# First up weights in two halves, weight blocks 4 to 7 one column at a time, and the deviation of two columns by a square root and a reciprocal

## The chip, the cores and the metric

The kernel runs on one core of a Trainium2 chip. The metric is the time on the device in microseconds (us), as the median of several runs. A profiled execution gives the trace of every instruction and DMA. The engines are TensorE (PE, matmuls; its weight loads are listed as PEld), VectorE (DVE), ScalarE (ACT), GpSimd (POOL) and SyncE (SP, which here only issues DMAs). Each engine works through its own instructions in the order of the program and waits at semaphores for the others.

## What is computed

A row of 512 numbers is normalised, and three things are added: the input, a spectral filter (a two-dimensional real FFT over 2048 rows and 512 columns, a product with a complex weight, and the inverse), and a gated feed-forward layer with 1792 hidden units. Cut to what matters:

```python
x = A_x                                   # 1 x 2048 x 512, bf16
xn = _layernorm(x)                        # (x - mean) / sqrt(var + 1e-5) along 512
g = einsum("bsd,df->bsf", xn, w_gate)     # w_gate, w_up: 512 x 1792
u = einsum("bsd,df->bsf", xn, w_up)
h = gelu(g) * u
out = x + irfft2(rfft2(xn) * (w_r + 1j * w_i)) + einsum("bsf,fd->bsd", h, w_down)
```

## The kernel before

The 2048 rows lie on 128 partitions in 16 columns of 128 rows each (`NC`); column `c` of the tile `x_t` is the rows 16p + c. For the feed-forward layer a column has to be normalised (`xn`), transposed (`xnT`, one tile for four columns, in four parts `e` of 128 of the 512 features), and multiplied by the gate weights `Wg_sb` and the up weights `Wu_sb`. The 1792 hidden units are 14 blocks of 128 (`f`). One gate or up product of a block for a column is four matmuls, one for each `e`.

The program isn't written down in the order in which it runs. Every step is entered in a plan (`_Plan`) with its engine, an assumed duration, what it depends on, and a due time (`prio`). `plan.run` simulates the engines with these assumed figures and, on every engine, takes next the step that is ready and has the smallest due time. Each load has an assumed landing time (`land=`). The order that comes out of this simulation is fixed in the program; on the chip only the waits are real. A changed assumption thus can change the order far behind the place that was edited.

What happens first:

- `load_x`, `load_ct`, `load_first`, `load_w` issue loads, nearly all from SP's queue, one after the other: x column 0, x column 1, the gate weights of blocks 0 to 3 in two halves (parts `e` 0, 1 from ACT's queue and 2, 3 from SP's, L339), the up weights of blocks 0 to 3 in one load (L348, 512 KB), the gate weights of blocks 4 to 7, x columns 2 and 3, the up weights of 4 to 7, then gate and up of 8 to 11 (512 KB each) and of 12 and 13 (256 KB each, L325), then x columns 4 to 7. `WD[f]` holds the loads that block `f` waits for. A load uses one of eight semaphores in turn, and waits for the load eight places before it.
- `dummies` puts matmuls of a constant tile `warm` on PE before the first real work: `NWARM` = 10 of them 512 wide (L387) and two of 128 behind the first transposes.
- `layernorm` of column 0, then column 1: DVE takes the statistics (L403, L410), adds epsilon (L411), POOL raises that to the power -0.5 (L417), DVE subtracts the mean and multiplies (L423), for these two columns in two halves of 256 features.
- `pe_transpose` (L437) transposes the two columns with matmuls against `ident`, and the result is copied from PSUM to `xnT` by ACT for the first half and by DVE for the second (L440). Columns 2 and on are transposed by DMAs (`dma_transpose`, L446).
- ACT loads the table of the gelu function at the very start, by a gelu of one number (L346).

Then the feed-forward layer: `glu(c0, n, f0, nf)` takes `n` columns and `nf` blocks: gate matmuls into a PSUM tile of the tag G, up matmuls into one of the tag U (two buffers each, L508), gelu of the gate by ACT into `ge` (L525), product with the up part by DVE into `hT` (L533). Matmuls in a call are sorted so that the parts `e` 0 and 1 come ahead of 2 and 3. The calls that matter here are

```python
    for c in range(2):
        glu(c, 1, 0, 4)
    for f in range(4, NFC, 2):
        glu(0, 2, f, 2)
    for f in range(0, NFC, 2):
        glu(2, 2, f, 2)
```

So columns 0 and 1 take the blocks 0 to 3 each by itself (matmuls 128 wide, 16 for the gate and 16 for up), and from block 4 on the two together, two blocks at a time (256 wide, 8 and 8). Then come columns 2 and 3, and from column 4 on four columns at once (512 wide), one block at a time.

Between these matmuls PE runs the filter: a fold and a first transform (`bp`, L591), for each of eight groups a transform along the features (`dp`, L634), a step over the columns (`ep`, L656), the filter on DVE (`filt`, ten to seventeen DVE operations), four DMAs on SP's queue that exchange halves of the result (`F` to `F2`, L760), and the step back (`gp`, L777). Each of those four DMAs has an assumed issue time and a lag in the plan. At the end the inverse along the features (`yp`, L828) and the down product (L882) give the output.

Of the kernel before, what the change touches and what calls it, by code (L numbers as in the profile page):

```python
# [10 lines left out]
P = 128  # L11
# [10 lines left out]
NE = 4  # L22
# [198 lines left out]
def kernel(  # L221
# [93 lines left out]
    def load_x(c0, n, land, eng="SP", deps=(), **kw):  # L315
        q = nc.sync if eng == "SP" else nc.scalar
        o = load(2 * n * P * D, lambda: q.dma_start(out=x_t[:, c0:c0 + n], in_=x_v[:, c0:c0 + n]), deps, eng=eng, land=land, **kw)
        for c in range(c0, c0 + n):
            XD[c] = o

    def load_w(f0, f1, lands, mid=lambda: None, deps=(), **kw):
        a, b = f0 * P, f1 * P
        os = []
        for t, v, land in ((Wg_sb, wg_v, lands[0]), (Wu_sb, wu_v, lands[1])):
            os.append(load(NE * P * P * (f1 - f0), lambda t=t, v=v: nc.sync.dma_start(out=t[:, :, a:b], in_=v[:, :, a:b]), deps, **kw,  # L325
                           land=land))
# [10 lines left out]
    def load_first(e, eng):  # L337
# [4 lines left out]
    load_x(0, 1, 3.15)  # L342
# [3 lines left out]
    add("ACT", 1.3, lambda: nc.scalar.activation(out=eps[:, 1:2], in_=eps[:, 0:1], func=AF.Gelu_apprx_tanh),  # L346
        (o_eps,), -900)
    d_u = load(NE * P * P * 4, lambda: nc.sync.dma_start(out=Wu_sb[:, :, 0:4 * P], in_=wu_v[:, :, 0:4 * P]), land=7.0)  # L348
    for f in range(4):
        WD[f] = [d_g, [d_u]]  # L350
    load_w(4, 8, (8.4, 10.9), lambda: load_x(2, 2, 9.6))
    load_w(8, 12, (12.2, 13.6))
    load_w(12, 14, (14.3, 15.0))
    load_x(4, 4, 17.3)
    g_idx = add("POOL", 0.8, lambda: nc.gpsimd.dma_start(out=idx_t[:], in_=idx_d), (), -10, lag=3.0)
    d_tw = []
# [22 lines left out]
    o_mem = [add("POOL", 0.3, lambda: nc.gpsimd.memset(warm[:], 1.0), (), -20, lag=0.05),  # L379
             add("POOL", 0.2, lambda: nc.gpsimd.memset(half[:], -0.5), (), -15, lag=0.05)]  # L380
    wb = _Buf("S")
    NWARM, NGAP, GAP = 10, 1, 2

    def warm_mm(w):
        if "warm" not in tiles:
# [19 lines left out]
    def layernorm(c0, n, due, after=(), halves=1):  # L405
# [6 lines left out]
            out=ve[:, k], in0=mv[:, k, 1], scalar1=EPS, scalar2=None, op0=ALU.add), ag, due - 5)  # L412
        normalize(c0, n, due, e, halves)

    def normalize(c0, n, due, e, halves, mean=None, op=ALU.subtract):
        k = slice(c0, c0 + n)
        r = add("POOL", 0.28 + 0.275 * n, lambda: nc.gpsimd.tensor_tensor(  # L417
            out=rstd[:, k], in0=ve[:, k], in1=half[:, k], op=ALU.pow), (e, o_mem[1]), due - 5, lag=0.1)
        for c in range(c0, c0 + n):
            XN[c] = []  # L420
            for h in range(halves):
                d = slice(h * D // halves, (h + 1) * D // halves)
                XN[c].append(dve(0.06 + 0.29 / halves, lambda c=c, d=d: V.tensor_scalar(  # L423
                    out=xn[:, c, d], in0=x_t[:, c, d], scalar1=mv[:, c, 0:1] if mean is None else mean,
                    scalar2=rstd[:, c:c + 1], op0=op, op1=ALU.mult), (r,), due - 2.5))

    def pe_transpose(c, due):
        XT[c] = []
        n = len(XN[c])
        for h in range(n):  # L430
            b = _Buf("S")
            es = range(h * NE // n, (h + 1) * NE // n)

            def mm(h=h, es=es):
                psum(f"tp.{c}.{h}", [P, NE, P], BF16)
                for e in es:
                    nc.tensor.transpose(tiles[f"tp.{c}.{h}"][:, e], xn[:, c, e * P:(e + 1) * P], ident)  # L437

            def ev(h=h, es=es, eng=(nc.scalar.copy, V.tensor_copy)[h]):
                eng(out=xnT[c // 4][:, es[0]:es[-1] + 1, c % 4], in_=tiles[f"tp.{c}.{h}"][:, es[0]:es[-1] + 1])  # L440

            o = pe(0.24 / n, mm, (XN[c][h], d_ident), due - 2, new=(b,))
            XT[c].append((act, dve)[h](0.1 + 0.35 / n, ev, (o,), due - 30, use=(b,)))

    def dma_transpose(c, due):
        XT[c] = [dma(320e3, lambda: nc.sync.dma_start_transpose(out=xnT[c // 4][:, :, c % 4], in_=xn[:, c]),  # L446
                    XN[c], due - 30, lag=1.0)]

    layernorm(0, 1, -28, (), 2)
    layernorm(1, 1, -25, (), 2)  # L450
    pe_transpose(0, -28)
    dummies(GAP, -29.9, XN[0], P)
    pe_transpose(1, -25)
    for c0, n, due in ((2, 2, -40), (4, 2, 14), (6, 2, 16), (8, 4, 24), (12, 4, 32)):
        layernorm(c0, n, due, XN[max(c0 - 4, 1)])
        for c in range(c0, c0 + n):
# [83 lines left out]
            HT.setdefault(c, []).append(h)  # L540
        return h

    for c in range(2):
        glu(c, 1, 0, 4)
    for f in range(4, NFC, 2):
        glu(0, 2, f, 2)
    for f in range(0, NFC, 2):
        glu(2, 2, f, 2)
# [118 lines left out]
    def filt(g, t):  # L667
# [87 lines left out]
        for h in range(2):  # L755
            for r in range(2):
                def mv_(h=h, r=r):
                    if h == 0 and r == 0:
                        work(f"F2.{g}", [P, 2, 2, 256], "F2")
                    nc.sync.dma_start(out=tiles[f"F2.{g}"][64 * r:64 * r + 64, h],  # L760
                                      in_=tiles[f"F.{g}"][64 * h:64 * h + 64, r])
                ex.append(dma(64 * 1024, mv_, [last] + ex[:1], t, new=(f2,) if not ex else (), use=(fb, f2), lag=1.0,
                              issue=0.1))
        FI_[g] = ex, f2

    def icstep(g, t):
# [170 lines left out]
```

## Time and profile before

| | |
|---|---|
| median of 9 runs | 178.88 us (178.46 to 179.12) |
| the profiled execution | 179.94 us |
| its span, first to last instruction | 178.2 us |
| PE busy | 172.5 us, 97% of the span |
| DVE, ACT, POOL busy | 119.0, 85.7, 17.4 us |
| PE's last matmul ends | 175.47 us |
| clock granted to PE | 1.00 |
| HBM read, written | 13.28 MB, 2.10 MB |

The span is shorter than the profiled execution's own time, since the latter holds the start and the end of the launch too. A busy time counts a stretch in which at least one instruction of the engine is under way; for PE this says that it was occupied, not that each matmul was as fast as it could be. In the lines from the trace that follow, a line in order of time gives the start, the duration, the engine, the line of the program, the operation, what it writes and reads, and in brackets how long the engine was idle before it and what ended that. `SPq` lines are the issue of a DMA, not its transfer; the view of a tile tells the time from issue to landing. A line of the view by stretch gives the stretch, its length, and the busy time and number of instructions of each engine, then the granted clock, the mean share of the 16 DMA engines that was busy, and what they moved in GB/s.

### The profile page before, as it was taken

Reading aid. Unit: us, or ns where it says so; the run is one execution under the profiler, and the core shown is the slowest. Engines: PE = TensorE matmul, PEld = TensorE weight load, DVE = VectorE, ACT = ScalarE, POOL = GpSimd, SP = SyncE. Lnnn points to the kernel's source line nnn. Section 1 sums busy time; section 2 is a strip of 40 time slices with the busy share of each in tenths; the row PEclk is TensorE's granted clock in tenths of the full one; section 3 lists DMA queues with packets and bytes.
Section 4 is the critical chain, followed back from the end, with each engine's and each line's share of the span. In section 5 each row is a group of like instructions: output and inputs, shape, how many; then the busy total and the mean of one; then the engine's idle time right before and its main releaser. Section 6 shows DMA issues by size and latency. Waiting matters only on the chain.

```text
span 178.2 us, 3153 instructions
## 1 busy us (share of the span) xinstructions
PE 172.5 (97%) x1154; PEld 98.3 (55%) x1154; DVE 119.0 (67%) x268; ACT 85.7 (48%) x156; POOL 17.4 (10%) x33
## 2 busy tenths in 40 slices
PE   6897999999999999999999999999999999999993
PEld 2696898754555454445454555444555444544463
DVE  2578999999853456999979998940066733632522
ACT  3222363463478984459989989540243211211100
POOL 3210021107871000000000000000000000000000
PEclk9999999999999999999999999999999999999999
DMA  5999864359958900012212211120004242222212
GB/s 142 347 358 249 282 136 81 70 131 247 224 140 273 343 6 0 0 43 61 48 30 60 58 48 47 30 59 4 0 0 146 80 131 90 88 74 73 61 60 59
DMA packets 23215, 19.51 MB, mean 110 GB/s; under 512 B 9568, under 2 KB 21856, under 8 KB 23200
## 3 DMA queue, kind: packets, MB, share of 16 engines
q1 hardware_dynamic: 22464, 17.84, 37.3%
q0 software_dynamic: 320, 1.19, 2.6%
q10 hardware_dynamic: 416, 0.30, 0.6%
q8 instruction: 9, 0.15, 0.4%
q14 instruction: 6, 0.05, 0.1%
HBM read 13.28 MB, written 2.10 MB: 86 GB/s over the span
## 4 chain that ended last, share of the span: by engine, by line
PE 87%; DMA 6%; SPq 2%; ACT 2%; issue 1%; DVE 0%
PE u_ps L508 24%; PE g_ps L508 24%; DMA Wu_sb<-in_B_w_up_dram 6%; PE bp L591 2%; PE yp L828 2%; PE gp L777 2%; PE ep L656 2%; PE dp L634 2%; PE yp__2132 L882 2%; PE yp__2079 L882 2%; PE yp__2048 L882 2%; PE yp__2021 L882 2%; PE yp__1990 L882 2%; PE yp__1902 L882 2%; PE yp__1870 L882 2%; PE yp__1835 L882 2%
## 5 line engine op out<-in xcount | busy, mean ns | idle before, releaser
L508 PE MATMUL u_ps<-xnT,Wu_sb 128*128 128x512 bf16 (+2 forms) x296 | 57.7, 327 | 1.3 <-DMA Wu_sb<-in_B_w_up_dram 1.3
L508 PE MATMUL g_ps<-xnT,Wg_sb 128*128 128x512 bf16 (+2 forms) x296 | 57.7, 327 | 0.2 <-ACT xnT L440 0.2
L525 ACT ACTIVATE ge<-g_ps 128x512 bf16<-128x512 f32 x56 | 33.5, 598 | 35.6 <-PE g_ps L508 32.6
L533 DVE TENSOR_TENSOR hT<-u_ps,ge 128x512 bf16<-128x512 f32 x56 | 38.3, 684 | 15.5 <-PE u_ps L508 13.7
L508 PEld LDWEIGHTS <-Wu_sb 128*128 128x128 bf16 x296 | 27.0, 98 | 20.0 <-DMA Wu_sb<-in_B_w_up_dram 1.9
L508 PEld LDWEIGHTS <-Wg_sb 128*128 128x128 bf16 x296 | 27.4, 98 | 19.2 <-issue 0.4
L882 PEld LDWEIGHTS <-hT 128*128 128x128 bf16 x252 | 23.1, 98 | 22.3
L834 ACT CAST yf<-yp 128x512 bf16<-128x512 f32 x16 | 8.9, 591 | 30.5 <-PE yp L828 30.5
L662 ACT CAST E<-ep 64x512 bf16<-64x512 f32 x32 | 18.5, 580 | 0.4
L850 DVE TENSOR_TENSOR lv<-yf 128x512 bf16<-128x512 bf16 x8 | 3.4, 423 | 16.0 <-ACT yf L834 15.6
L403 DVE BATCH_NORM_STATS2 st<-x_t 128x6 f32<-128x512 bf16 x16 | 10.8, 672 | 3.7 <-DMA x_t<-in_A_x_dram 3.7
L783 ACT CAST Gs<-gp 128x512 bf16<-128x512 f32 x16 | 8.7, 594 | 7.0 <-PE gp L777 7.0
L639 ACT CAST ds<-dp 128x512 bf16<-128x512 f32 x16 | 9.0, 587 | 1.5 <-PE dp L634 1.5
L417 POOL TENSOR_TENSOR rstd<-ve,half 128x2 f32<-128x2 f32 (+2 forms) x7 | 5.6, 803 | 33.8 <-DVE ve L411 33.8
L595 ACT CAST Bs<-bp 128x512 bf16<-128x512 f32 x16 | 8.4, 600 | 1.0 <-PE bp L591 1.0
L423 DVE TENSOR_SCALAR xn<-x_t,mv,rstd 128x512 bf16<-128x512 bf16 (+1 forms) x18 | 6.4, 398 | 0.2 <-POOL rstd L417 0.2
L828 PEld LDWEIGHTS <-Gs 128*128 128x128 bf16 x64 | 4.6, 98 | 2.8
L387 PE MATMUL warm<-warm 128*128 128x512 bf16 (+1 forms) x12 | 4.7, 562 | 1.3 <-POOL half L380 1.3
L634 PEld LDWEIGHTS <-Bs 128*128 128x128 bf16 x64 | 4.5, 98 | 2.4
L777 PEld LDWEIGHTS <-F 128*128 128x128 bf16 x64 | 4.4, 98 | 2.3 <-issue 0.2
L693 DVE TENSOR_TENSOR m<-X,TW 128x1024 bf16<-128x1024 bf16 x8 | 5.5, 692 | 0.2
L828 PE MATMUL yp<-CT,Gs 128*128 128x128 bf16 x64 | 5.5, 219 | 0.0
(103 smaller groups left out, 170.6 us busy)
## 6 DMA issues: line engine op xcount, KB each, us to landing
y<-in_A_x_dram SPq DMA_DIRECT2D x16, 128.0 KB, 2.3
F<-F SPq DMA_DIRECT2D x32, 64.0 KB, 2.0
out_dram<-y SPq DMA_DIRECT2D x15, 128.0 KB, 1.7
Wd_sb<-in_B_w_down_dram SPq DMA_DIRECT2D x1, 1792.0 KB, 8.8
Wu_sb<-in_B_w_up_dram SPq DMA_DIRECT2D x3, 512.0 KB, 7.9
x_t<-in_A_x_dram SPq DMA_DIRECT2D x3, 512.0 KB, 6.2
Wg_sb<-in_B_w_gate_dram SPq DMA_DIRECT2D x2, 512.0 KB, 7.8
Wg_sb<-in_B_w_gate_dram SPq DMA_DIRECT2D x2, 256.0 KB, 7.2
```

Source lines behind the costliest of these rows:

```text
L403: V.bn_stats(out=st[:], in_=x_t[:, c])
L508: nc.tensor.matmul(tiles[f"{nm}.{key}"][:, f * w:f * w + w], lhsT=W[:, e, (f0 + f) * P:(f0 + f + 1) * P], rhs=rhs(e), start=(f + e == 0), ...
L525: nc.scalar.activation(out=e[:, 0:nf * w], in_=tiles[f"g_ps.{key}"][:, 0:nf * w], func=AF.Gelu_apprx_tanh)
L533: V.tensor_tensor(out=out, in0=tiles[f"u_ps.{key}"][:, 0:nf * w].rearrange("p (f w) -> p f w", w=w) if nf > 1 else tiles[f"u_ps.{key}"][:, ...
L595: nc.scalar.copy(out=o, in_=tiles[f"bp.{cg}.{q}"][:].rearrange("p c (r g a) -> p (c r) g a", r=2, a=4))
L634: nc.tensor.matmul(dp[:, q % 2, q // 2], lhsT=Bs[:, q, G].rearrange("p c r a -> p (c r a)"), rhs=FQ[q], start=(q == 0), stop=(q == 3), ski ...
L639: nc.scalar.copy(out=ds[:].rearrange("p (s k t) -> p s k t", s=2, t=2), in_=tiles[f"dp.{G}"][:].rearrange("p s t k -> p s k t"))
L662: nc.scalar.copy(out=tiles[f"E.{g}"][64 * h:64 * h + 64, r], in_=tiles[f"ep.{g}.{h}"][64 * r:64 * r + 64])
L783: nc.scalar.copy(out=o, in_=tiles[f"gp.{g}.{h}"][:].rearrange("p q (n a) -> p (q n) a", a=4))
L828: nc.tensor.matmul(yp[:, q], lhsT=tiles["G"][:, q, c], rhs=IQ[q], start=(q == 0), stop=(q == 3), skip_group_check=True)
L834: nc.scalar.copy(out=tiles[f"yf.{c // 2}"][:, c % 2], in_=tiles[f"yp.{c}"][:])
L882: nc.tensor.matmul(y[:, s], lhsT=tiles[sb, f][:, cl * P:(cl + 1) * P], rhs=Wd_sb[:, f, s], start=(f == 0), stop=False)
```

## The change

Five things are changed.

1. The up weights of blocks 0 to 3 are loaded in two halves of 256 KB, parts `e` 0 and 1 and parts 2 and 3. The gate weights of blocks 8 to 13 become one load of 768 KB (before: 8 to 11 and, two loads later, 12 and 13); the up weights of 8 to 11 and of 12 and 13 follow it. The assumed landings are changed along with it.
2. Columns 0 and 1 take the blocks 4 to 7 each by itself, like the blocks 0 to 3.
3. For columns 0 and 1 the reciprocal of the deviation comes from a ScalarE square root (with epsilon as its bias) and a VectorE reciprocal. ACT's first table is that of the square root, and the gelu table is loaded behind the second square root. The statistics of column 1 are put behind the normalising of column 0 on DVE.
4. The transposed column 1 is copied from PSUM by DVE alone; eight warm matmuls instead of ten.
5. The plan's assumed issue time of the exchange DMAs in the filter goes from 0.1 to 0.5 and their lag from 1.0 to 0.8. These are only figures of the plan.

```diff
-    add("ACT", 1.3, lambda: nc.scalar.activation(out=eps[:, 1:2], in_=eps[:, 0:1], func=AF.Gelu_apprx_tanh),
-        (o_eps,), -900)
-    d_u = load(NE * P * P * 4, lambda: nc.sync.dma_start(out=Wu_sb[:, :, 0:4 * P], in_=wu_v[:, :, 0:4 * P]), land=7.0)
+    add("ACT", 1.5, lambda: nc.scalar.activation(out=eps[:, 1:2], in_=eps[:, 0:1], func=AF.Sqrt), (o_eps,), -900)
+    d_u = [load(P * P * 16, lambda e=e: nc.sync.dma_start(out=Wu_sb[:, e:e + 2, 0:4 * P], in_=wu_v[:, e:e + 2, 0:4 * P]),
+                land=(6.9, 7.3)[e // 2]) for e in (0, 2)]
     for f in range(4):
-        WD[f] = [d_g, [d_u]]
+        WD[f] = [d_g, d_u]
     load_w(4, 8, (8.4, 10.9), lambda: load_x(2, 2, 9.6))
-    load_w(8, 12, (12.2, 13.6))
-    load_w(12, 14, (14.3, 15.0))
+    d_g = [load(NE * P * P * 6, lambda: nc.sync.dma_start(out=Wg_sb[:, :, 8 * P:14 * P], in_=wg_v[:, :, 8 * P:14 * P]),
+                land=13.2)]
+    for a, b, land in ((8, 12, 14.3), (12, 14, 15.3)):
+        d_u = [load(NE * P * P * (b - a), lambda a=a * P, b=b * P: nc.sync.dma_start(
+            out=Wu_sb[:, :, a:b], in_=wu_v[:, :, a:b]), land=land)]
+        for f in range(a, b):
+            WD[f] = [d_g, d_u]
...
-    NWARM, NGAP, GAP = 10, 1, 2
+    NWARM, NGAP, GAP = 8, 1, 2
...
+    def layernorm_sqrt(c, due, prev=()):
+        s = dve(0.65, lambda: stats(c), [XD[c]] + list(prev), due - 3.0)
+        a = dve(0.18, lambda: V.bn_aggr(out=mv[:, c], in_=tiles["st", c][:]), (s,), due - 3.2)
+        r = SD[c] = act(0.25, lambda: nc.scalar.activation(
+            out=rstd[:, c:c + 1], in_=mv[:, c, 1:2], func=AF.Sqrt, bias=eps[:, 0:1], scale=1.0), (a, o_eps), due - 60)
+        r = dve(0.12, lambda: V.reciprocal(out=rstd[:, c:c + 1], in_=rstd[:, c:c + 1]), (r,), due - 3.0)
+        XN[c] = []
+        for h in range(2):
+            d = slice(h * 256, h * 256 + 256)
+            XN[c].append(dve(0.24, lambda d=d: V.tensor_scalar(
+                out=xn[:, c, d], in0=x_t[:, c, d], scalar1=mv[:, c, 0:1], scalar2=rstd[:, c:c + 1],
+                op0=ALU.subtract, op1=ALU.mult), (r,), due - 2.5))
...
-    layernorm(0, 1, -28, (), 2)
-    layernorm(1, 1, -25, (), 2)
+    layernorm_sqrt(0, -28)
+    layernorm_sqrt(1, -25, XN[0])
     pe_transpose(0, -28)
     dummies(GAP, -29.9, XN[0], P)
-    pe_transpose(1, -25)
+    act(1.5, lambda: nc.scalar.activation(out=eps[:, 1:2], in_=eps[:, 0:1], func=AF.Gelu_apprx_tanh), [SD[1]] + XT[0], -70)
+    pe_transpose(1, -25, 1)
...
-    for c in range(2):
-        glu(c, 1, 0, 4)
-    for f in range(4, NFC, 2):
+    for f in (0, 4):
+        for c in range(2):
+            glu(c, 1, f, 4)
+    for f in range(8, NFC, 2):
         glu(0, 2, f, 2)
...
-                ex.append(dma(64 * 1024, mv_, [last] + ex[:1], t, new=(f2,) if not ex else (), use=(fb, f2), lag=1.0,
-                              issue=0.1))
+                ex.append(dma(64 * 1024, mv_, [last] + ex[:1], t, new=(f2,) if not ex else (), use=(fb, f2), lag=0.8,
+                              issue=0.5))
```

More of the change, by code (lines that the diff above doesn't have):

```diff
@@ L340, in load_first @@
                     land=5.1)
-    load_x(0, 1, 3.15)
+    load_x(0, 1, 3.2)
     d_ident = load_ct("ident", "ident", "ACT", land=2.9)
@@ L413, in layernorm @@
         normalize(c0, n, due, e, halves)
+    SD = {}
+    def layernorm_sqrt(c, due, prev=()):
[10 more added lines that the diff above has]
+                op0=ALU.subtract, op1=ALU.mult), (r,), due - 2.5))
     def normalize(c0, n, due, e, halves, mean=None, op=ALU.subtract):
@@ L425, in normalize, with pe_transpose @@
                     scalar2=rstd[:, c:c + 1], op0=op, op1=ALU.mult), (r,), due - 2.5))
-    def pe_transpose(c, due):
+    def pe_transpose(c, due, k=0):
         XT[c] = []
@@ L437, in mm, with ev @@
                     nc.tensor.transpose(tiles[f"tp.{c}.{h}"][:, e], xn[:, c, e * P:(e + 1) * P], ident)
-            def ev(h=h, es=es, eng=(nc.scalar.copy, V.tensor_copy)[h]):
+            def ev(h=h, es=es, eng=(nc.scalar.copy, V.tensor_copy)[h or k]):
                 eng(out=xnT[c // 4][:, es[0]:es[-1] + 1, c % 4], in_=tiles[f"tp.{c}.{h}"][:, es[0]:es[-1] + 1])
             o = pe(0.24 / n, mm, (XN[c][h], d_ident), due - 2, new=(b,))
-            XT[c].append((act, dve)[h](0.1 + 0.35 / n, ev, (o,), due - 30, use=(b,)))
+            XT[c].append((act, dve)[h or k](0.1 + 0.35 / n, ev, (o,), due - 30, use=(b,)))
     def dma_transpose(c, due):
```

## The prediction

> **What bounds the kernel now.** I read the busy times by stretch first, then the waits of TensorE (PE), then the first 22 us in order of time, then what each load took to land.
>
> ```profile
> core 0: us, PE busy (x) PEld busy (x) DVE busy (x) ACT busy (x) POOL busy (x), PEclk, DMA share, GB/s
> 45.00:55.00 10.00, 10.00 (x71) 5.50 (x70) 6.73 (x11) 6.49 (x13) 7.47 (x16) 1.00 0.71 174
> 88.00:96.00 8.00, 8.00 (x56) 4.35 (x55) 6.88 (x16) 7.32 (x15) 0.00 (x0) 1.00 0.26 62
> ```
>
> ```profile
> PE u_ps L508 <- DMA Wu_sb<-in_B_w_up_dram: 1.3, 2, 0.9
> PE g_ps L508 <- ACT xnT L440: 0.2, 1, 0.2
> ```
>
> From 16.29 us to its last matmul PE never stands still for more than 0.1 us, so the middle offers nothing to win. All idle time that an edit can touch lies in the head: 0.23 us before 6.46, 0.36 before 8.10, 0.90 before 16.29. Everything behind 16.29 is a packed queue, so the end moves by as much as the matmul that starts there, unless a new wait opens later. I call it U8: the first `u_ps` matmul of weight blocks 8 and 9.
>
> ```profile
> 4.91 2.06 SPq L325 DMA_DIRECT2D Wu_sb<-in_B_w_up_dram  x1
> ...
> 7.01 1.76 SPq L325 DMA_DIRECT2D Wg_sb<-in_B_w_gate_dram  x1
> ...
> 8.10 1.07 PE L508 MATMUL u_ps<-xnT,Wu_sb 128*128 128x128 bf16 x16 [0.36 <-DMA Wu_sb<-in_B_w_up_dram]
> ...
> 14.36 1.04 PE L508 MATMUL g_ps<-xnT,Wg_sb 128*128 128x256 bf16 x8
> ...
> 16.29 1.05 PE L508 MATMUL u_ps<-xnT,Wu_sb 128*128 128x256 bf16 x8 [0.90 <-DMA Wu_sb<-in_B_w_up_dram]
> ...
> 20.67 1.04 PE L508 MATMUL g_ps<-xnT,Wg_sb 128*128 128x256 bf16 x8
> ```
>
> U8 starts 0.05 us after its weights, the up blocks 8 to 11, land: the issue at 4.91 takes 11.3 us to its landing, which is 16.24 by the semaphore's records.
>
> ```profile
> DMA to landing us min/median/max: 11.3/11.3/11.3
> ```
>
> The loads in order land at 6.13 (second gate half), 8.05 (up 0-3), 9.45 (gate 4-7), 10.17 (x columns 2, 3), 11.68 (up 4-7), 13.19 (gate 8-11), 16.24 (up 8-11), 16.94 (gate 12, 13), 17.67 (up 12, 13). Each 512 KB takes 1.40 to 1.51 us behind its forerunner, each 256 KB 0.70 to 0.73, except the one that decides, which takes 3.05. A landing has 16 parts, one for each DMA engine. Of up 8-11 fifteen are there by 14.44 and the last comes 1.80 us later. The packet records show why that can be: at 14.04 one 16,384-byte packet of queue q8 (nine of kind "instruction" in the run) starts and takes 1.16 us, on an engine whose queue of weights is full. These packets follow PE's place in its program: the first comes at about PE's 231st record, the next at 434, 688, 948.
>
> So U8 hangs on the landing of up 8-11 on one engine that is some 1.8 us late.
>
> **The change, part by part.**
>
> Loads. Before up 8-11 the new order puts one load of gate 8-13 (768 KB) where gate 8-11 (512 KB) was; gate 12, 13 move ahead of up 8-11. Up 8-11 thus has 256 KB more in front of it. Price: 0.70 (gate 12, 13) to 0.76 us (half of the 1.51). These are the bytes that were in by 16.94 before: I take 16.90 to 17.00 for the new landing. SP issues twelve loads up to x columns 4-7, as before (up 0-3 are now two, gate 8-13 is now one). The added issue of some 0.5 us lies at 2.6, and from 4.91 on SP was held back anyway (2.06, 1.76, 1.60 us for issues that otherwise take 0.5), so the DMA engines don't run dry.
>
> Up weights in halves. Their first half should land near 7.1 (6.13 plus half of the 1.92 to 8.05), the second at 8.05 as before. A split could cost something by itself; the 256 KB loads issued at 7.01 and 8.81 land 0.73 us apart, which is about half of the 1.51 for 512 KB, so I take nothing. The Trainium skill (DMA: Bandwidth & Descriptors, Anatomy of one DMA) speaks against splitting: about 2.0 us fixed for each DMA. Paid in line, that would put the second half at about 10 and U8, by PE's own path, near 17.1 rather than 16.95; the landings 0.73 us apart contradict it for queued loads.
>
> Deviation of columns 0 and 1. Before: VectorE (DVE) adds epsilon, POOL takes a power, DVE normalises from 5.05.
>
> ```profile
> 2.98 0.20 ACT L346 ACTIVATE eps<-eps 128x1 f32<-128x1 f32 x1
> ...
> 4.12 0.15 DVE L411 TENSOR_SCALAR ve<-mv 128x1 f32<-128x1 f32 x1
> ...
> 4.43 0.58 POOL L417 TENSOR_TENSOR rstd<-ve,half 128x1 f32<-128x1 f32 x1 [2.38 <-DVE ve L411]
> ...
> 5.05 0.60 DVE L423 TENSOR_SCALAR xn<-x_t,mv,rstd 128x256 bf16<-128x256 bf16 x2
> ```
>
> The new chain is a ScalarE (ACT) square root on 128x1 and a DVE reciprocal. Neither is in the trace. The root lies between 0.20 (the 128x1 activation) and 0.37 (a 128x256 copy); I take 0.20. The reciprocal lies between 0.15 (128x1) and 0.18 (aggregate); I take 0.15. With hops of 0.1: aggregate ends 4.09, root 4.2 to 4.4, reciprocal to 4.65, normalising from 4.65. That is 0.40 earlier (0.2 at the dear ends), and gate column 0 starts at 6.05 rather than 6.46. Column 1's chain is put behind column 0's and ends near 7.5, well before its transposes.
>
> ACT tables. A second table load (1.28 us, the row at 1.69) follows the second root: 6.7 to 8.0, the first gelu ends at 8.8 rather than 8.15. Covered: the `g_ps` buffer that it frees is next asked for near 10.4. The Trainium skill (ScalarE: Activation LUTs, What ACT_TABLE_LOAD costs) adds 1.38 us of draining, which the row at 2.98, straight behind the load, doesn't show. With it the gelu would end at 10.2, still in time, so the sum is the same by both.
>
> PE's order. The built program runs gate c0, up c0, transposes c1, gate c0 of blocks 4-7, gate c1, up c1, up c0, gate c1, up c1 of 4-7, then blocks 8, 9. A unit of 16 matmuls 128 wide takes 0.89 (8.10 to 9.01 and on), one of 8 of 256 takes 0.87: four units at 0.02 more are 0.08. By landings: gate 6.05 to 6.95; up held at its second half, 8.05, done 8.55; transposes to 8.95; gate 4-7 waits for 9.45, done 10.36; five units more to 14.8. PE would reach gate 8 at 14.8 (before: 14.36) and U8 at 15.67. Gate c1 no longer waits for its transposed column, since that is copied under gate 4-7. Leaving out two warm matmuls (0.43 each) costs nothing: the eighth is done near 4.8, before the transposes can start.
>
> Clock. The transposes start 107 ns apart up to 5.80 and 56 from 5.90: PE gets to full pace at about 5.85. With two warm matmuls less there is a hole of some 0.3 us before that. Should full pace come later, gate c0 takes 16 x 0.051 = 0.82 more; PE's own path would then end near 16.1, still under the landing.
>
> Columns 2 and 3. DVE has two products ahead of their normalising, which ends near 14.45 rather than 13.65; the transposing DMAs land at 19.57 and 19.97, so up to 20.8. Their reader starts at 20.67, then at 21.3. Cover 0.5 us.
>
> Middle. The planner reorders the filter groups. The gp matmuls come later in PE's order or at the same place; they stood 2.8 us or more behind their landings before, and PSUM buffers were free 0.78 us or more before their next writer. I take 0, with 0 to 0.3 for the range.
>
> Sum: the late engine's records repeat if the instruction packet falls again while it still has up 8-11 ahead. PE's 231st record is now at the second gate unit of column 1, blocks 4-7, near 13.0, so yes. Gate 8-13 lands at 15.4, gate 8 runs to 16.3, U8 starts at 16.95: +0.66 us. The span would be 178.2 + 0.66 = 178.9. The profiled execution took 179.94, 1.74 over its span and 1.06 over the median of the runs; I carry the difference over: 178.88 + 0.66 = 179.5.
>
> **Rivals.**
>
> The engine isn't late. Should it be under 0.6 us late in the new order, or in runs without the profiler, PE's own path sets U8: 15.67, -0.62, 178.3. It becomes a gain when up 8-11 lands before 16.24. For it: fifteen engines had up 8-11 by 14.44. Against: the instruction packet comes earlier in the new order, with more bytes behind it; and columns 2 and 3 would then be wanted at 20.05, with landings of 19.97 to 20.8.
>
> Nothing comes through. The earlier start and the later landing cancel: the 0.40 us of the root chain are swallowed by the wait for 8.05 (in the sum above they are), and the extra 256 KB fall into the time the late engine loses anyway. U8 at 16.2 to 16.4, 178.9. Against: the landings are in order of bytes.
>
> Columns 2 and 3 come late. DVE's two extra products delay the transposes by more than the cover; from a landing of 21.3 on, each us costs one. At a delay of 0.8 for DVE plus 1.0 in the queue behind the last x load (landed 19.03) that is 21.8: 0.5 on top of 0.66, 180.0.
>
> **How the numbers follow.** Chances: forecast 0.55 (own range 179.2 to 179.7, from the price of 256 KB, the middle's 0.3 and the landing records), late columns 0.10, nothing 0.12, engine not late 0.23. The predicted time is 179.5. The range runs from 178.2 (the gain) to 180.0 (the late columns) since the cases have both signs. This kernel's measurement tells about 0.2% from no change, 0.36 us. Slower 0.63 (forecast but its lowest 0.02, and late columns), within 0.2% 0.14, faster 0.23.
>
> **What would show it.** Right: U8 waits for the up weights until 16.8 to 17.0; gate 8 waits too, to about 15.4; column 0 normalised from 4.65 and gate c0 from 6.05; no wait of PE behind U8. Wrong: U8 at 15.7 with no wait (the engine was on time), a wait of `g_ps` on `xnT` near 21, a PE gap in the filter stretch, or gate c0 at 107 ns pace.

## The result, and the profile after

The changed kernel takes 180.03 us (median of 18 runs, 179.34 to 180.77) against 178.89 for the kernel before in the same rounds: a ratio of 1.0066 [1.0055, 1.0076], 1.14 us slower. The execution profiled took 180.16 us, its span is 178.4 us.

First the waits of PE in the changed kernel (what waited, for what, us in total, times, longest).

```profile
PE warm L392 <- POOL half L385: 1.3, 1, 1.3
PE g_ps L529 <- DMA Wg_sb<-in_B_w_gate_dram: 0.7, 1, 0.7
PE tp L457 <- DVE xn L431: 0.4, 1, 0.4
PE bp L613 <- DMA RF_t<-spec_rf: 0.3, 1, 0.3
```

The wait for the up weights is gone, and two others are there: of a gate unit for the gate weights of blocks 4 to 7, and of the first filter step `bp` for `RF_t`, the constants of its transform. Where they stand is seen in the order of time:

```profile
3.51 0.69 DVE L408 BATCH_NORM_STATS2 st<-x_t 128x6 f32<-128x512 bf16 x1 [3.51 <-DMA x_t<-in_A_x_dram]
...
4.46 0.29 ACT L425 ACTIVATE rstd<-mv,eps 128x1 f32<-128x1 f32 x1 [1.26 <-DVE mv L424]
4.78 0.16 DVE L427 RECIPROCAL rstd<-rstd 128x1 f32<-128x1 f32 x1 [0.36 <-ACT rstd L425]
4.98 0.60 DVE L431 TENSOR_SCALAR xn<-x_t,mv,rstd 128x256 bf16<-128x256 bf16 x2
...
6.24 1.12 PE L529 MATMUL g_ps<-xnT,Wg_sb 128*128 128x128 bf16 x16
...
6.81 1.28 ACT L473 ACT_TABLE_LOAD   x1
...
8.11 0.20 ACT L473 ACTIVATE eps<-eps 128x1 f32<-128x1 f32 x1
8.22 0.58 ACT L546 ACTIVATE ge<-g_ps 128x512 bf16<-128x512 f32 x1
...
9.71 1.96 PE L529 MATMUL g_ps<-xnT,Wg_sb 128*128 128x128 bf16 x32 [0.65 <-DMA Wg_sb<-in_B_w_gate_dram]
...
14.11 0.73 DVE L443 TENSOR_SCALAR xn<-x_t,mv,rstd 128x512 bf16<-128x512 bf16 x2
...
14.54 3.30 SPq L466 DMA_TRANSPOSE xnT<-xn  x2
...
15.96 1.04 PE L529 MATMUL u_ps<-xnT,Wu_sb 128*128 128x256 bf16 x8
...
17.89 0.57 SPq L317 DMA_DIRECT2D x_t<-in_A_x_dram  x1
...
18.52 0.42 SPq L481 DMA_DIRECT2D RF_t<-spec_rf  x1
...
24.25 0.94 PE L613 MATMUL bp<-RF_t,xf 128*128 128x128 bf16 x14 [0.28 <-DMA RF_t<-spec_rf]
```

U8 starts at 15.96 and waits for nothing. It is where it is because the gate unit at 9.71 waited for its weights, and seven units of 0.89 us lie between the two (9.71 + 6.25 = 15.96). Further on, `bp` waits 0.28 us for a transfer issued at 18.52. SP issues in order: the load of `RF_t` stands behind the two transposes of columns 2 and 3 and behind an x load, and these stand behind the normalising at 14.11. The view of `RF_t` has its time from issue to landing:

```profile
DMA to landing us min/median/max: 5.7/5.7/5.7
```

So it lands at 24.21, and `bp` starts. Behind it the list above has no wait of PE, and the view by stretch shows full occupation as before:

```profile
core 0: us, PE busy (x) PEld busy (x) DVE busy (x) ACT busy (x) POOL busy (x), PEclk, DMA share, GB/s
45.00:55.00 10.00, 10.00 (x72) 5.52 (x71) 6.82 (x11) 6.46 (x14) 7.57 (x16) 1.00 0.90 180
88.00:96.00 8.00, 8.00 (x51) 4.13 (x49) 7.83 (x18) 7.60 (x15) 0.00 (x0) 1.00 0.17 41
```

The start of `bp` is the best single mark for what follows: it stands behind all the work of the head, and from it to the last matmul it takes 151.31 or 151.32 us in every profile of a kernel with neither the new deviation nor the new plan figures, 151.44 in the changed one.

### The profile page after: what moved, and what is told of

Same layout as the page of the kernel before. It is cut to its first block, busy times and chain, and to the rows that moved or that the text cites. A ratio compares the mean times of both kernels' runs of the same rounds, so it can differ in the third digit from the quotient of the medians.

```text
span 178.4 us, 3214 instructions
## 1 busy us (share of the span) xinstructions
PE 172.5 (97%) x1184; PEld 98.5 (55%) x1184; DVE 119.4 (67%) x269; ACT 87.6 (49%) x159; POOL 16.3 (9%) x31
## 4 chain that ended last, share of the span: by engine, by line
PE 85%; DMA 7%; DVE 2%; ACT 2%; SPq 2%; issue 1%
PE g_ps L529 23%; PE u_ps L529 23%; DMA Wg_sb<-in_B_w_gate_dram 4%; DMA RF_t<-spec_rf 3%; PE ep L678 2%; PE bp L613 2%; PE yp L850 2%; PE gp L799 2%; PE yp__2137 L904 2%; PE yp__2110 L904 2%; PE yp__2021 L904 2%; PE yp__1994 L904 2%; PE yp__1963 L904 2%; PE yp__1933 L904 2%; PE yp__1747 L904 2%; PE yp__2163 L904 2%
## 5 line engine op out<-in xcount | busy, mean ns | idle before, releaser
L529 PEld LDWEIGHTS <-Wu_sb 128*128 128x128 bf16 x312 | 27.6, 98 | 19.5 <-DMA Wu_sb<-in_B_w_up_dram 0.6
L872 DVE TENSOR_TENSOR lv<-yf 128x512 bf16<-128x512 bf16 x8 | 3.4, 423 | 16.5 <-ACT yf L856 16.2
L437 POOL TENSOR_TENSOR rstd<-ve,half 128x2 f32<-128x2 f32 (+1 forms) x5 | 4.5, 902 | 35.0 <-DVE ve L416 35.0
L715 DVE TENSOR_TENSOR m<-X,TW 128x1024 bf16<-128x1024 bf16 x8 | 5.5, 692 | 0.2
L721 DVE TENSOR_TENSOR m<-X,TW 128x1024 bf16<-128x1024 bf16 x8 | 5.5, 685 | 0.0
L799 PE MATMUL gp<-CT,F 128*128 128x128 bf16 x64 | 5.4, 219 | 0.0
```

The source lines that it names most:

```text
L529: nc.tensor.matmul(tiles[f"{nm}.{key}"][:, f * w:f * w + w], lhsT=W[:, e, (f0 + f) * P:(f0 + f + 1) * P], rhs=rhs(e), start=(f + e == 0), ...
L799: nc.tensor.matmul(gp[:, q], lhsT=F[:, h, q % 2, q // 2::2], rhs=cc("M" if 2 * g + h else "M0"), start=(q == 0), stop=(q == 3), skip_group ...
```

## The experiments

Each kernel's diff is against the kernel before or the changed kernel, as said. Ratios are to the kernel before in the same rounds, with a 95% interval; they differ from the quotient of the medians by up to 0.3%, most where the runs spread.

**The kernel before once more** (no edit), since the prediction was built on an execution that took 179.94 us.

> The kernel before, unchanged, for a second profile. The first profiled execution took 179.94 us, the median is 178.89. Theory T1 (the first profile was an unusual one: the instruction packet fell on the engine that still had the up weights of blocks 8 to 11 ahead, and in most executions it does not): the new profile has a span near 177.1 us, U8 (the first u_ps matmul of blocks 8 and 9) starts near 15.2, without the 0.90 us wait. Rival (profiling itself costs the 1.06 us and the late engine is always there): the span is 178.2 again and U8 starts at 16.2 to 16.3.

Measured: 178.81 us, 1.001 [0.9989, 1.0032]. Its profiled execution took 178.75 us, with a span of 176.9. The only wait listed for PE is that of the first warm matmul:

```profile
PE warm L387 <- POOL half L380: 1.3, 1, 1.3
```

In order of time:

```profile
12.43 0.73 DVE L423 TENSOR_SCALAR xn<-x_t,mv,rstd 128x512 bf16<-128x512 bf16 x2 [0.22 <-POOL rstd L417]
...
12.87 3.66 SPq L446 DMA_TRANSPOSE xnT<-xn  x2
...
14.74 1.04 PE L508 MATMUL u_ps<-xnT,Wu_sb 128*128 128x256 bf16 x8
...
16.58 0.57 SPq L317 DMA_DIRECT2D x_t<-in_A_x_dram  x1
...
17.21 0.42 SPq L460 DMA_DIRECT2D RF_t<-spec_rf  x1
...
22.92 1.05 PE L591 MATMUL bp<-RF_t,xf 128*128 128x128 bf16 x16
```

Here U8 starts at 14.74 and waits for nothing, 1.55 us earlier than in the execution of the prediction, and `bp` at 22.92 rather than 24.16. This is the ordinary execution: the median of the kernel before lies within 0.2 us of it. Between U8 and `bp` PE has two small holes, 0.18 us ahead of the gate unit at 19.29 and 0.14 ahead of `bp`; `RF_t`, issued at 17.21, lands just in time.

The landings that matter, read from the semaphores' records, with the first 16,384-byte packet of kind "instruction" (us):

```
                          prediction's  before again  new loads alone  changed
instruction packet               14.04         13.59            13.24    14.96
gate 4-7 land                     9.45          8.95             9.09     9.67
  fifteen parts of them           9.19          8.94             8.74     9.35
up 8-11 land                     16.24         14.22            16.15    15.51
  fifteen parts of them          14.44         14.16            14.90    15.24
U8 starts                        16.29         14.74            16.20    15.96
RF_t issued                      17.64         17.21            16.87    18.52
bp starts                        24.16         22.92            24.07    24.25
```

In the ordinary execution up 8-11 are complete, on all engines, while the packet is still under way: that engine had done its share of them. The load that the packet hits is the next one, gate 12, 13: fifteen parts by 15.07, the last at 16.05, and nobody waits for it. The two executions also differ before any such packet: in the prediction's, one part of each load from up 0-3 to gate 8-11 is already 0.25 to 0.27 us behind the other fifteen; in this one it is at most 0.07.

**The new loads alone**, in the kernel before. The orders of PE, DVE and ACT are those of the kernel before; only the loads differ.

```diff
-    d_u = load(NE * P * P * 4, lambda: nc.sync.dma_start(out=Wu_sb[:, :, 0:4 * P], in_=wu_v[:, :, 0:4 * P]), land=7.0)
+    d_u = [load(P * P * 16, lambda e=e: nc.sync.dma_start(out=Wu_sb[:, e:e + 2, 0:4 * P], in_=wu_v[:, e:e + 2, 0:4 * P]),
+                land=(6.9, 7.3)[e // 2]) for e in (0, 2)]
...
-    load_w(8, 12, (12.2, 13.6))
-    load_w(12, 14, (14.3, 15.0))
+    d_g = [load(NE * P * P * 6, lambda: nc.sync.dma_start(out=Wg_sb[:, :, 8 * P:14 * P], in_=wg_v[:, :, 8 * P:14 * P]),
+                land=13.2)]
...
```

> The kernel before with only the new load order; the orders of PE, DVE and ACT are those of before to the instruction, so U8 would be ready at about 14.7. Theory Q1 (up 8-11 behind gate 8-13 now lies behind the 16 KB instruction packet, and lands at 16.0 to 16.2 on the last engine; with the old order it had landed before the packet came): U8 waits 0.8 to 1.4 us, 179.4 to 180.1 us. Rival Q0 (the load order is not on the path): 178.8 to 179.1.

Measured: 179.75 us, 1.0033 [1.0011, 1.0055]. Two of ten runs took 178.72 and 178.80, eight 179.65 to 180.24. The profiled one (179.89), in order of time:

```profile
13.94 1.04 PE L514 MATMUL g_ps<-xnT,Wg_sb 128*128 128x256 bf16 x8
...
16.20 1.05 PE L514 MATMUL u_ps<-xnT,Wu_sb 128*128 128x256 bf16 x8 [1.22 <-DMA Wu_sb<-in_B_w_up_dram]
...
24.07 1.06 PE L597 MATMUL bp<-RF_t,xf 128*128 128x128 bf16 x16
```

This shows the first cost by itself. Fifteen of the sixteen parts of up 8-11 are in by 14.90, 0.74 us later than in the kernel before again (14.16), as forecast for 256 KB; but that is late enough for the packet at 13.24 to catch one engine, whose part comes 1.25 us after the others. U8 waits 1.22 us. The two quick runs are as quick as the kernel before; that the engine isn't caught in them is likely, but neither was profiled.

**The new order of blocks alone**, in the kernel before.

```diff
-    for c in range(2):
-        glu(c, 1, 0, 4)
-    for f in range(4, NFC, 2):
+    for f in (0, 4):
+        for c in range(2):
+            glu(c, 1, f, 4)
+    for f in range(8, NFC, 2):
```

> The kernel before with only blocks 4 to 7 of columns 0 and 1 taken one column at a time. Theory O: gate 4-7 comes up one unit later than in the changed kernel and column 1's transposes stand in their old place, so the loads are in: 179.0 to 179.3 us. Rival B: 179.5 to 180.0, with normalising of column 2 near 13.4 rather than 12.4 and a wait of bp for RF_t.

Measured: 179.87 us, 1.0049 [1.0031, 1.0067]. In the profiled execution (179.36, half a us under the median) columns 2 and 3 are normalised from 13.65 (12.43 in the kernel before again), U8 starts at 15.51 after a wait of 0.2 us for gate 4-7, and `bp` starts 0.63 us later than in the kernel before again:

```profile
18.03 0.42 SPq L460 DMA_DIRECT2D RF_t<-spec_rf  x1
...
23.55 1.05 PE L592 MATMUL bp<-RF_t,xf 128*128 128x128 bf16 x16
```

`RF_t` lands at 23.51, 0.19 us after the turn of `bp` (the matmul ahead starts at 23.26, and these follow each other in 0.11). So 0.44 of the 0.63 us are PE's own path, and 0.19 the wait for `RF_t`. The same with the load of `RF_t` moved ahead of the x load in SP's queue:

```diff
-            load_x(8, 4, 0.0, deps=XN[3], prio=-80.0)
...
+            load_x(8, 4, 0.0, deps=XN[3], prio=-80.0)
```

> The kernel before with blocks 4 to 7 one column at a time and RF_t issued ahead of x columns 8 to 11. Theory Q2 (one column at a time puts a product more ahead of the normalising of columns 2 and 3 on DVE, that holds SP's transposes, x 8 to 11 and RF_t back, and bp waits for RF_t): 0.3 to 0.8 us less than the blocks alone (179.87), so 179.0 to 179.5, and no wait of bp. Rival (the loss of the blocks is elsewhere in the head): 179.7 to 180.0.

Measured: 179.13 us, 1.0014 [0.9999, 1.0029]; `RF_t` lands at 21.66, and `bp` starts without a wait:

```profile
17.49 0.57 SPq L459 DMA_DIRECT2D RF_t<-spec_rf  x1
...
23.27 1.06 PE L592 MATMUL bp<-RF_t,xf 128*128 128x128 bf16 x16
```

Swapping two entries of SP's queue thus takes 0.74 us off the median, three quarters of this part's cost (0.97 us over the kernel before in its rounds, then 0.22). That is the second cost, and it goes by way of SP's queue. The two profiles show 0.28 us of it (`bp` at 23.55 and 23.27); the rest lies in runs that weren't profiled.

**The new deviation alone**, in the kernel before (square root, reciprocal and second table load; copies and warm matmuls as before).

```diff
-    layernorm(0, 1, -28, (), 2)
-    layernorm(1, 1, -25, (), 2)
+    layernorm_sqrt(0, -28)
+    layernorm_sqrt(1, -25, XN[0])
...
+    act(1.5, lambda: nc.scalar.activation(out=eps[:, 1:2], in_=eps[:, 0:1], func=AF.Gelu_apprx_tanh), [SD[1]] + XT[0], -70)
```

> The kernel before with only the square root and reciprocal for columns 0 and 1 (and the gelu table loaded behind them). PE's order stays, but DVE has one product more ahead of the normalising of columns 2 and 3. Theory R (this part costs by itself: column 1's chain is later, and columns 2 and 3 are normalised later, so RF_t comes later): 179.2 to 179.5 us. Rival G (the earlier start of column 0 is a gain once the other parts are gone): 178.5 to 178.8.

Measured: 179.65 us, 1.0041 [1.002, 1.0062]. The profiled execution is one of its slowest (180.6), and shows the second cost again, larger. In order of time:

```profile
13.60 0.73 DVE L437 TENSOR_SCALAR xn<-x_t,mv,rstd 128x512 bf16<-128x512 bf16 x2
...
18.41 0.42 SPq L475 DMA_DIRECT2D RF_t<-spec_rf  x1
...
24.46 0.72 PE L606 MATMUL bp<-RF_t,xf 128*128 128x128 bf16 x10 [1.09 <-DMA RF_t<-spec_rf]
```

The planner has put one more product `hT` ahead of the normalising of columns 2 and 3 on DVE. From `bp` to the last matmul it takes 151.66 us, 0.35 more than in the kernel before, with a wait of 0.2 of the filter step `ep` for ACT. So of the 0.61 us between the medians (179.65 and 179.04) about half would be the middle, in another order; the time is just above what was expected for a cost of this part.

**The new deviation, the halves, and `RF_t` first**, in the kernel before: the loads' order of blocks 8 to 13 stays old.

```diff
-    d_u = load(NE * P * P * 4, lambda: nc.sync.dma_start(out=Wu_sb[:, :, 0:4 * P], in_=wu_v[:, :, 0:4 * P]), land=7.0)
+    d_u = [load(P * P * 16, lambda e=e: nc.sync.dma_start(out=Wu_sb[:, e:e + 2, 0:4 * P], in_=wu_v[:, e:e + 2, 0:4 * P]),
...
+    layernorm_sqrt(0, -28)
+    layernorm_sqrt(1, -25, XN[0])
...
-            load_x(8, 4, 0.0, deps=XN[3], prio=-80.0)
...
+            load_x(8, 4, 0.0, deps=XN[3], prio=-80.0)
```

> The kernel before with the new deviation, up 0-3 in halves (the other loads as before) and RF_t first: the parts that could bring the start forward, without those that cost. Rival G: 178.3 to 178.7 us, faster than before with RF_t first alone (178.76). Theory R: 178.9 to 179.3.

Measured: 180.01 us, 1.0061 [1.0036, 1.0085]: no gain, and over both expectations. The profiled execution took 179.82, 1.07 more than the kernel before again. `bp` starts without a wait at 23.25 (0.33 later); from there to the last matmul it takes 151.66 us (0.34 more); and 3.13 us pass from the last matmul to the end of the span rather than 2.70 (0.42 more). Of the 0.34, PE's waits show 0.2:

```profile
PE ep L672 <- ACT ds L655: 0.2, 1, 0.2
```

So here the cost isn't in the head alone: the planner's order of the middle is another one, and PE's step `ep` waits for ACT. The 0.42 at the end belong to the kernel. It issues one load more than the kernel before (two halves, and nothing merged), so the last store of the output uses another of the eight semaphores. At the end SP waits for the semaphores in a fixed order, 0.06 us from one to the next. In the sixteen other executions profiled, the last store's comes last, the rest are passed while it is under way, and 2.70 to 2.71 us go by from the last matmul to the end. Here and in the next kernel it comes ahead of seven others, which are passed only after it landed. SP's wait for the store is longer by as much; the lines are of `RF_t` first alone (shown further on), of this kernel, and of the next:

```profile
SPq L932 <- DMA out_dram<-y: 0.6, 1, 0.6
...
SPq L948 <- DMA out_dram<-y: 1.0, 1, 1.0
...
SPq L933 <- DMA out_dram<-y: 1.0, 1, 1.0
```

In the changed kernel the merged load of gate 8-13 brings the number back, and the end takes 2.70.

**The halves and `RF_t` first**, in the kernel before, without the deviation (the first and the last part of the diff above).

> The kernel before with up 0-3 in halves and RF_t first, old deviation. If halves let the first up product start before all of up 0-3 is in, where one engine is late: 178.5 to 178.75 us. If they bring nothing: 178.7 to 178.85, as RF_t first alone.

Measured: 179.34 us, 1.0015 [0.9999, 1.0032]: over both expectations, and 0.58 us over `RF_t` first alone (178.76). 0.42 of that is the end just described. The profiled execution (179.89, one of the three slowest) shows something else besides: the packet comes at 13.18, fifteen parts of up 8-11 are in by 14.28 and the last at 15.72, with the old order of the loads.

```profile
15.77 1.05 PE L509 MATMUL u_ps<-xnT,Wu_sb 128*128 128x256 bf16 x8 [0.79 <-DMA Wu_sb<-in_B_w_up_dram]
```

So the new order of the loads isn't needed for this wait; an earlier packet does it too. Loading the up weights in halves brings no gain here.

**`RF_t` first alone**, in the kernel before: two entries of SP's queue swapped.

> The kernel before with RF_t issued ahead of x columns 8 to 11 and nothing else; only two entries of SP's queue change places. In the second profile of before bp started 0.07 after the time at which RF_t should land, 0.14 us behind the last up matmul. If Q2's chain also sets the kernel before: 178.6 to 178.85, up to 0.3 us less. If not: 178.8 to 179.0.

Measured: 178.76 us (178.38 to 179.03), 0.9988 [0.9975, 1.0002]. It is the quickest kernel of all, but the interval holds 1. In order of time:

```profile
12.51 0.73 DVE L423 TENSOR_SCALAR xn<-x_t,mv,rstd 128x512 bf16<-128x512 bf16 x2 [0.21 <-POOL rstd L417]
...
16.11 0.57 SPq L459 DMA_DIRECT2D RF_t<-spec_rf  x1
...
22.80 1.06 PE L591 MATMUL bp<-RF_t,xf 128*128 128x128 bf16 x16
```

`RF_t` is issued 1.10 us earlier than in the kernel before again, and `bp` gains 0.12: what was left of its wait.

**Parts taken out of the changed kernel.** Blocks 4 and on in pairs again, as in the kernel before:

```diff
-    for f in (0, 4):
-        for c in range(2):
-            glu(c, 1, f, 4)
-    for f in range(8, NFC, 2):
+    for c in range(2):
+        glu(c, 1, 0, 4)
+    for f in range(4, NFC, 2):
```

> The changed kernel with blocks 4 to 7 of columns 0 and 1 together again, 256 wide, all else as changed. T1 (PE's new order meets the gate weights of blocks 4 to 7 before they land, 0.65 us of idle time in the profile of after, and all five units behind it shift): 179.3 to 179.6 us, and no wait of PE for gate 4-7. Rival M (the loss lies in the filter stretch, by the plan's new figures): 180.0, unchanged.

Measured: 179.31 us, 1.0027 [1.0005, 1.005]. Seven of twelve runs are at 179.02 to 179.32, the rest at 179.91 to 180.75. The profiled one is of the second kind (180.02): up 8-11 land at 16.17, fifteen parts by 15.27, with the packet at 13.94; U8 starts at 16.22, `bp` at 24.09. The order of blocks is the part whose removal helps most.

The plan's old figures for the exchange DMAs (`lag=1.0`, `issue=0.1`):

> The changed kernel with the exchange DMAs' plan figures back at issue 0.1 and lag 1.0. The head is the same, the filter stretch in another order. T1: 179.9 to 180.1 us, no change. Rival M: the loss goes, 178.9 to 179.3.

Measured: 179.69 us, 1.0044 [1.0027, 1.006]. From `bp` to the last matmul it takes 151.32 us as in the kernel before, against 151.44 in the changed kernel: the figures cost 0.12 us. Neither expectation held, and the rest of the difference to the changed kernel lies in the head (`bp` at 23.88); the intervals overlap.

The old loads, as in the kernel before (the diff of the new loads alone, reversed):

> The changed kernel with the old loads: up 0-3 in one, gate and up of 8 to 11, then of 12 and 13. T1 (PE's order is the cause): 179.9 to 180.3 us, since gate 4-7 lands when it did and up 0-3 not earlier. Rival L (the 256 KB in front of up 8-11 are the cause, as forecast): 179.3 to 179.5.

Measured: 180.33 us, 1.0082 [1.0051, 1.0113], so no gain. Three of the six runs are at 179.47 to 179.91, three at 180.76 to 181.33. The profiled one is of the first kind (179.57): U8 starts at 15.23, but `bp` waits 0.25 us for `RF_t` and starts at 23.51, and to the last matmul it takes 151.58.

The old deviation (the diff of the new deviation alone, reversed):

> The changed kernel with the deviation of columns 0 and 1 by POOL's power again (one gelu table at the start, column 1's statistics not held back); the other parts stay. PE's order is then gate, transposes c1, up, gate c1, up c1, and only then blocks 4 to 7, each column by itself. Theory O (what costs is that column 1's late chain moved its transposes and its gate unit behind other units, so that PE meets loads before they land): 178.9 to 179.3 us, U8 near 14.8 to 14.9, no wait for gate 4-7. Rival B (128 wide blocks 4 to 7 are the cost in themselves, by the two products more that DVE has ahead of columns 2 and 3): 179.6 to 180.0.

Measured: 180.33 us, 1.0066 [1.0042, 1.009], so no gain either, and neither expectation held: up 8-11 land at 16.15, U8 starts at 16.20 after a wait of 0.47, `bp` at 24.07.

`RF_t` ahead of the x load:

> The changed kernel with the load of RF_t issued ahead of x columns 8 to 11 instead of behind. In the profile of after bp waited 0.3 us for RF_t, and 0.6 in the run with the old plan figures. If that wait is a term of the loss: 0.3 to 0.6 us less than the changed kernel on the same chip, and no wait of bp. If it only takes the place of another (columns 8 to 11 late): the same time within 0.1.

Measured: 179.93 us, 1.005 [1.0032, 1.0068]. The wait for `RF_t` is gone, and U8 waits 0.69 us for up 8-11, which land at 16.06; `bp` starts at 23.97. The time is 0.31 us under that of the changed kernel in the same rounds (180.24), and the intervals overlap, so neither expectation is settled. Both, old loads and `RF_t` first:

> The changed kernel with the old loads and RF_t ahead of x columns 8 to 11, so that both waits are gone. Q1 and Q2 together: 179.0 to 179.4 us, U8 at 15.1 to 15.4 without a wait, bp 7.9 to 8.0 behind it. If either half is wrong: 179.7 or more.

Measured: 179.55 us, 1.0039 [1.002, 1.0059], between the two expectations. `bp` doesn't wait, but starts at 23.77: in this execution up 0-3, now whole, landed at 8.17 (fifteen parts by 7.45), and the first up unit waited 0.91 us. And with the old deviation as well:

> The changed kernel with old loads, RF_t first and the old deviation; left are the up halves gone too, blocks 4 to 7 by column, eight warm matmuls and the plan's new figures. The run with old loads and RF_t first still stood 0.64 us above before. Theory R: this falls to 179.1 to 179.3. Rival (the rest is the plan's figures and the blocks): 179.5 to 179.6, as it was.

Measured: 180.69 us, 1.0058 [1.0032, 1.0084], with runs from 179.09 to 181.84. In the profiled one a single part of every load is late: fifteen parts of up 12, 13 are in by 16.09 (15.85 in the kernel before again), the last at 18.50 (16.83), and U8 starts at 17.07. Neither expectation held, and the spread lets nothing be read from it.

**The changed kernel once more:**

> The changed kernel, unchanged, on the chip of the next three. 179.8 to 180.2 us; U8 between 15.2 (loads on time) and 16.0 (late), PE waiting for gate 4-7 and for RF_t.

Measured: 180.24 us, 1.0065 [1.004, 1.0091]. U8 starts at 15.81, gate 4-7 are waited for 0.51 us, `RF_t` is issued at 18.26, `bp` starts at 23.97: the picture of the first profile, but for the first gate unit, which takes 1.81 us instead of 1.12:

```profile
5.85 1.81 PE L529 MATMUL g_ps<-xnT,Wg_sb 128*128 128x128 bf16 x16
```

## Why the prediction was wrong in its size

The direction was right, and the kernel is slower by 1.14 us where 0.66 were forecast. But it was not right by its own path, and so in part by luck: the wait that the forecast hangs on, of U8 for up 8-11, is in neither profile of the changed kernel. It is in those of three kernels that differ from it in one part (pairs again, old deviation, `RF_t` first: 0.83, 0.47 and 0.69 us). Point by point:

1. **The base: the step that failed.** The sum started from an execution with U8 at 16.29 and a late engine, and carried "1.06 over the median of the runs" over, as if it lay outside the span. It lay inside: in all runs here the time is 1.7 to 1.9 us over its span. The ordinary execution of the kernel before has a span of 176.9, U8 at 14.74 and no wait there. A profile 0.6% over a median whose runs lie within 0.4% was the sign. Against the ordinary base U8 moves by 1.22 us (14.74 to 15.96), not by 0.66, and it doesn't wait there: PE's own path ends at 15.96, and `bp` then waits for `RF_t`.

2. **The late engine.** That an instruction packet sets one engine's weights back, and that 256 KB more lie ahead of up 8-11, was right, and so was the price of the bytes (0.70 to 0.76; the new loads alone show 0.74). What was missed: in the kernel before these weights are usually through when the packet comes, and the 0.74 us are what puts them behind it. The cost is the shadow of the packet, in the new loads alone a wait of 1.22 us. Gate 8-13 land at 13.3 to 14.2, not at 15.4, and hold up nothing; up 8-11 at 14.8 to 16.2, not at 16.9. That the late engine's records would repeat in the changed kernel was the forecast's second wrong step: the packet came at PE's 292nd and 306th record in its two profiles (14.96 and 15.43), not at the 231st (near 13.0), and up 8-11 landed at 15.51 and 15.68. So the packet doesn't follow PE's place alone.

3. **PE's own path** to U8 was forecast as 15.67; it is 15.96 and 15.81 in the two profiles, with the forecast wait for gate 4-7 (9.67 rather than 9.45). The prediction took this path for covered, and in its first rival for a gain of 0.62. Against 14.74 it is a loss: the new order asks for gate 4-7 one gate and one up unit of column 1 earlier, at 9.06, where the kernel before again asks at 10.21. In the eighteen executions profiled gate 4-7 land between 8.73 and 10.10. That start would cover all of them; the changed kernel lets much of the difference through. The first up unit, too, stands still before each of its halves, 0.27 and 0.29 us in the first profile.

4. **Columns 2 and 3.** That DVE would come to them later was seen; the delay is 1.68 us (12.43 to 14.11) where 0.8 was written. It was followed only to the reader of the transposed columns, with "cover 0.5 us", and not along SP's queue to the load behind, of `RF_t`, which goes from 17.21 to 18.52 and which `bp` waits for. The rival of late columns named this delay, but with the wrong reader. In the kernel before `RF_t` has no cover (a hole of 0.14 us ahead of `bp`), so a delay there comes through: with the blocks alone, whose own path is 0.44 us longer, `bp` still waits 0.19 for it.

5. **Two chains of like length.** U8 at 15.8 to 16.2 and `RF_t` near 24 each put `bp` at 23.5 to 24.3. This would explain why taking out the loads, the deviation or the wait for `RF_t` gives back little or nothing, and why the parts alone (1.0033, 1.0049, 1.0041) add up to more than the whole (1.0066). It is argued, not shown: with the old loads and `RF_t` first, neither chain should bind, and 0.64 us remain. And the deviation alone has 0.35 us of another order in the middle, which the whole doesn't have.

6. **The deviation** behaves as worked out: from the statistics' start to the normalising it takes 1.47 us (3.51 to 4.98), as forecast (3.18 to 4.65), and 1.87 before. The root took 0.29, the reciprocal 0.16. The 0.40 us are gained and swallowed, as forecast: gate column 0 starts at 6.24 rather than 6.05 (in this execution the statistics start 0.33 us later), up waits and then gate 4-7 wait. The first gelu ends at 8.80, as forecast, with the second table load of 1.28 us covered. What the prediction didn't see is that the planner, fed with it, delays columns 2 and 3 and, where nothing else is changed, reorders the middle: alone it costs 0.41%, about half of it in the middle.

   The drain that the Trainium skill (ScalarE: Activation LUTs, What ACT_TABLE_LOAD costs) adds to a table load doesn't show here either: the load ends at 8.09, the next activation starts at 8.11.

7. **Halves free**: right for the landings. They are 0.75 us apart (7.42, 8.17) in the changed kernel and 0.69 in the new loads alone (6.58, 7.27), where the whole load came at 7.47. The 2.0 us fixed for each DMA that the Trainium skill (DMA: Bandwidth & Descriptors, Anatomy of one DMA) gives, in a section on DMAs issued by GpSimd, don't show between these loads from SP's queue. But no run shows a gain, and where nothing is merged in return, the further load costs 0.42 us at the end.

8. **Middle**: 0.12 us, inside the 0 to 0.3 allowed, and due to the plan's figures. **Clock**: in the first profile PE idles 0.45 us before the transposes, where 0.3 were expected, and still runs the first gate unit at 56 ns from matmul to matmul. In the second it idles 0.06, and the unit runs at 107 ns up to 7.37, the pace that the prediction named as a sign of being wrong. The granted clock is 1.00 in both. The slow unit costs next to nothing there: its last matmul starts at 7.43, and the first up half lands at 7.41. The hole and the pace don't go together in these two.

The sum that fits the two profiles: `bp` 1.33 us later (22.92 to 24.25), the middle 0.12 longer; together 1.45, which is the difference of the spans (176.94 and 178.39). Of the 1.33, the wait for `RF_t` takes 0.44, counted from the turn of `bp` (23.71 and 0.11), and PE's own path the rest. The medians differ by 1.14.

**Open.** Why in some executions one part of every load is late from the first loads on (0.72 us for up 0-3 with the old loads and `RF_t` first, 0.01 in the kernel before again), and why the packet comes when it does; the 0.64 us by which that kernel stays above the kernel before (its middle is 0.27 longer, the rest is in the head, in one execution); and with it how the 1.14 us of the medians divide among the parts.

## What to carry to other kernels

Set the profiled execution's time against the median before anything is added up: if it is over by more than the runs spread, its largest wait may be the disturbance itself, and the change must be priced on an ordinary execution. When a producer comes later, follow it through every queue in which something stands behind it, to the last reader: here two products on VectorE delayed a load of constants by way of two transposes in SyncE's queue. Where a transfer ends just in time, moving its issue past a neighbour is a cheap test; and where two chains end within a few tenths of a us, a part taken out alone need not show its price. Count the DMAs, too, when semaphores go round: one load more moved the end by 0.42 us.

## What the runs showed of the hardware

Instruction packets of 16,384 bytes share the DMA engines with the kernel's loads. Those looked at took 0.9 to 1.6 us (1.16 in the new loads alone). Where one shows in a load in flight, one part of the load came 0.9 to 1.8 us behind the other fifteen (1.25 there, 0.98 for gate 12, 13 in the kernel before again). It doesn't always show: in the first profile of the changed kernel the packet at 14.96 took 1.17 us with up 8-11 and up 12, 13 in flight, and their last parts came 0.27 and 0.29 us behind, as in the load before (0.29). The Trainium skill (Runtime: NRT & Kernel Launch, Instruction fetch mechanics) calls the cost of such a refill mostly hidden; in the new loads alone it is not: PE waits 1.22 us for the sixteenth part.

A kernel whose path hangs on such a landing can have times in two groups, as with the new loads alone (178.72 and 178.80, then 179.65 and up), while the kernel before, whose landing is early by half a us, was over 179.5 in only two of its ten runs when measured once more.
